# Attention followed by a routed expert layer: the gathers of later experts placed ahead of the flushed weight loads, one tile turned by TensorE

## The chip, the cores and the metric

One core of one Trainium2 chip runs the whole program. The metric is the device time of one execution in microseconds; the median of three executions is compared. The profile is of one further execution of the same program.

## What is computed

The reference is attention with normalised queries and keys, followed by a layer of eight experts to which every token is sent by a hash of its id:

```python
q_n, k_n = rmsnorm(q, g_q), rmsnorm(k, g_k)           # q, k, v: 8 x 12 x 448 x 64
attn = softmax(q_n @ k_n.T / 8) @ v
x = attn.transpose(0, 2, 1, 3).reshape(3584, 768)
expert_idx = token_ids * 2654435761 % 8
for e in range(8):
    mask = expert_idx == e
    h = np.maximum(x[mask] @ w1[e], 0.0)               # w1[e]: 768 x 1024
    out[mask] = h @ w2[e]                              # w2[e]: 1024 x 768
```

## The kernel before

The first half is attention. It writes x to a scratch tensor in DRAM (x_scratch), and beside it the token table gidx is made: for each expert up to 480 row numbers in four tiles (three of 128 rows, the last of 96).

The second half, from some 160 us on, goes through the experts in order, in the loop at line 1264. For an expert e it does the following.

- Gather: `fetch` (line 1048) issues one indirect DMA on GpSimd for each of the four tiles, from x_scratch into a ring of eight slots in SBUF (kr in the profile, line 230). Experts of even number use slots 0 to 3, those of odd number 4 to 7. Expert 2 is fetched inside expert 0's second product (line 1248), expert e + 2 at the head of expert e's turn through the loop (line 1274).
- Turn: the rows must stand with the model dimension on the partitions. For experts 2 to 6 VectorE does it, in `turn_blocks` (line 1061, the instructions are on line 1072) with sixteen 32-row block transposes: twelve of 32 x 768 and four of 32 x 576, since the last tile has 96 rows. They are issued for expert e + 1 ahead of expert e's first product. Experts 0 and 1 are turned tile by tile by TensorE (`turn`, line 1055, and `put_xT`, line 238: six transposes to PSUM and one copy back), expert 7 by DMA transposes on SyncE (line 1080).
- First product, `gemm1` (line 991; matmuls on line 1002, the ReLU on ScalarE on line 1011): 48 matmuls of 480 columns.
- Second product, `gemm2` (line 1018; matmuls on line 1024): four tiles of 16 matmuls, each copied out of PSUM on line 1034 and scattered to the output by an indirect DMA on GpSimd (line 1037).
- Weights: `w_pieces` (line 1083) cuts an expert's weights into three pieces of w1 (512 KB each in SBUF) and two of w2 (768 KB each), and `w_next` (line 1102) issues the next ones on GpSimd (line 1105). At the end of expert e the rest of the queue is issued and the pieces of expert e + 4 are queued. For e of 1 and more two pieces are issued after the first product and one after each tile of the second; for e = 0 one each after tiles 2 and 3, and three at the end.

GpSimd carries out its instructions in the order in which they are written, so the order of gathers, weight pieces and scatters in the program is the order in which they are issued. The two halves are scheduled by hand: what the plans `plan`, `before` and `between` (lines 1244 to 1258) name for an expert and a tile is issued at that place. The weights of expert e + 4 use the buffers of expert e; two buffers hold turned rows of experts 1 to 7, and a separate one those of expert 0.

Of the kernel before, what the change touches and what calls it, by code (L numbers as in the profile page):

```python
# [20 lines left out]
def kernel(  # L21
# [16 lines left out]
    E = moe_w1.shape[0]  # L38
# [13 lines left out]
    LAST = FIT - 3 * P  # L52
    KT = CAP // P
# [175 lines left out]
    def gather(xg, idx, rows=N):  # L229
        nc.gpsimd.indirect_dma_start(  # L230
            out=xg[0:idx.shape[0], :], out_offset=None, in_=x_dram[0:rows, :],
            in_offset=bass.IndirectOffsetOnAxis(ap=idx, axis=0),
            bounds_check=rows - 1, oob_is_err=False)
        return xg
# [729 lines left out]
    with tc.manual_schedule(), \  # L964
# [10 lines left out]
        def w1_view(e, w1_sb):  # L975
            return w1_sb[:].rearrange("p c (o f) -> p c o f" if e == 0 else "p c (f o) -> p c o f",
                                      o=FO)
# [13 lines left out]
        def gemm1(w1v, xT, h_sb, c0, c1, both=True, after=(), apart=0):  # L991
            banks = {}

            def products(fo, a0, a1):
                if fo not in banks:
                    banks[fo] = ps_h.tile([P, 512], FP32, name="h_ps")
                dst = banks[fo][:, a0 - c0:a1 - c0]
                if xT is xT_e:
                    dst = dst.rearrange("p (k t) -> p k t", t=P)
                for co in range(CO):  # L1000
                    src = xT[:, a0 // P:a1 // P, co, :] if xT is xT_e else xT[:, co, a0:a1]
                    nc.tensor.matmul(dst, lhsT=w1v[:, co, fo, :], rhs=src,  # L1002
                                     start=(co == 0), stop=(co == CO - 1))

            for fo in range(apart):
                products(fo, c0, c1 - P)
            for fo in range(FO):
                products(fo, c1 - P if fo < apart else c0, c1)
                h_ps = banks.pop(fo)
                if fo % 2 == 0 or not both:  # L1010
                    nc.scalar.activation(h_sb[:, fo, c0:c1], h_ps[:, :c1 - c0], AF.Relu)  # L1011
                else:
                    nc.vector.tensor_scalar(out=h_sb[:, fo, c0:c1], in0=h_ps[:, :c1 - c0],
                                            scalar1=0.0, scalar2=None, op0=ALU.max)
                for f in after[fo] if after else ():
                    f()
# [31 lines left out]
        def fetch(e, kts):  # L1048
            for kt in kts:
                c = e * KT + kt  # L1050
                xgs[c] = gather(xg_ring[:, c % (2 * KT)],
                                gidx[0:P if kt < KT - 1 else LAST, c:c + 1],
                                N_EARLY if kt < KT - 1 else N)

        def turn(e, kt, copy=None):
            if e not in xTs:
                xTs[e] = m_x.tile([P, CO, CAP], FP16, name="xT")
            bank = ps_x.tile([P, DIN], FP16, name="xT_ps")
            put_xT(xgs.pop(e * KT + kt), xTs[e], kt, bank[:], copy)

        def turn_blocks(e):
            xT = xTs[e] = m_x.tile([P, CO, CAP], FP16, name="xT")
            c0 = e * KT % (2 * KT)
            xg = xg_ring[:, c0:c0 + KT].rearrange("p k (c m r) -> p k m c r", m=4, r=32)
            dst = xT[:].rearrange("p c (g r) -> p c g r", r=32)
            for kt in range(KT):
                xgs.pop(e * KT + kt)
            for i in range(4):
                n = KT if 32 * i < LAST else KT - 1
                g = slice(i, i + 4 * (n - 1) + 1, 4)  # L1070
                for m in range(4):
                    nc.vector.transpose(  # L1072
                        out=dst[32 * m:32 * m + 32, :, g].rearrange("p c k r -> p k c r"),
                        in_=xg[32 * i:32 * i + 32, 0:n, m])

        def turn_by_dma(e):
            xTs[e] = m_x.tile([P, CO, CAP], FP16, name="xT")
            for kt in range(KT):
                n = P if kt < KT - 1 else LAST
                nc.sync.dma_start_transpose(out=xTs[e][:, :, kt * P:kt * P + n],  # L1080
                                            in_=xgs.pop(e * KT + kt)[0:n, :])
# [20 lines left out]
        def w_next(n):  # L1102
            for _ in range(min(n, len(queue))):
                o, i = queue.pop(0)
                nc.gpsimd.dma_start(out=o, in_=i)  # L1105
# [135 lines left out]
        def each(f, *parts):  # L1241
            return [lambda p=p: f(p) for p in parts]
# [3 lines left out]
            (0, "g", 4): [p7, p8], (0, "g", 5): [p9, p10, p11],  # L1246
            (0, "g", 6): each(low, 0, 1), (0, "g", 7): each(low, 2, 3), (0, "k", 0): [high],
            (0, "k", 1): [high_tok], (0, "k", 2): [table_mm, lambda: fetch(2, range(KT))],
            (1, "k", 0): [overflow_table],
        }  # L1250
        t = lambda e, kt: (lambda: turn(e, kt))
        t0 = lambda e, kt: (lambda: turn(e, kt, nc.scalar.copy))
        before, between = {}, {}
# [2 lines left out]
        before[0, 2] = [lambda: gemm1_late(w1_view(0, w_tiles[0][0]), xTs.pop(0), hs[0], EARLY, FIT)]  # L1256
        between[0, 2] = t0(1, 2)
        before[0, 3] = [t(1, 3)]
        hs = {}
        fetch(0, [KT - 1])  # L1260
        fetch(1, [KT - 1])
# [2 lines left out]
        for e in range(E):  # L1264
            w1_sb, w2_sb = w_tiles[e]
            h_sb = hs[e] = m_h.tile([P, FO, CAP], FP16, name="h_sb")
            after = [plan.get((e, "g", fo), []) for fo in range(FO)]
            if e == 0:
                gemm1(w1_view(e, w1_sb), xTs[e], h_sb, 0, EARLY, False, after, 2)
            else:  # L1270
                if e == E - 2:
                    turn_by_dma(E - 1)
                if e < E - 2:
                    fetch(e + 2, range(KT))
                    turn_blocks(e + 1)
                gemm1(w1_view(e, w1_sb), xTs.pop(e), h_sb, 0, FIT, e >= E - 2, after)
            if e:
                w_next(2)
            if e == 2:
                n_ov = nc.values_load(novi[0:1, 0:1], min_val=0, max_val=NOV)  # L1280
            if e == E - 1:
                nc.gpsimd.drain()
            for kt in range(KT):
                c = e * KT + kt
                for f in before.get((e, kt), []):
                    f()
                gemm2(w2_sb, h_sb, kt, gidx[:, c:c + 1], between=between.get((e, kt)),
                      last=(c == E * KT - 1), by_v=e in (0, E - 2, E - 1))
                for f in plan.get((e, "k", kt), []):
                    f()  # L1290
                if e or kt > 1:
                    w_next(1)
            w_next(len(queue))
            if e + 4 < E:
                queue += w_pieces(e + 4)
# [47 lines left out]
```

## Time and profile before

| | us |
|---|---|
| median of 3 runs | 331.68 |
| lowest and highest | 331.52, 332.45 |
| the profiled execution | 332.74 |
| its span, first to last instruction | 331.1 |

| engine | busy, us | share of the span |
|---|---|---|
| TensorE, matmuls | 318.2 | 96% |
| VectorE | 239.3 | 72% |
| ScalarE | 207.5 | 63% |
| GpSimd | 149.5 | 45% |

The 1.6 us by which the profiled execution is longer than its span lie ahead of the first and behind the last instruction. TensorE's busy time is modelled at the ends of matmuls, so 96% is not 96% of its peak; its granted clock is 0.994 over the span. The shares are means over the attention and the expert phase, whose limits differ; the change lies in the second.

### The profile page before, as it was taken

Reading aid. Unit: us, or ns where it says so; the run is one execution under the profiler, and the core shown is the slowest. Engines: PE = TensorE matmul, PEld = TensorE weight load, DVE = VectorE, ACT = ScalarE, POOL = GpSimd, SP = SyncE. Lnnn points to the kernel's source line nnn. Section 1 sums busy time; section 2 is a strip of 40 time slices with the busy share of each in tenths; the row PEclk is TensorE's granted clock in tenths of the full one; section 3 lists DMA queues with packets and bytes.
Section 4 is the critical chain, followed back from the end, with each engine's and each line's share of the span. In section 5 each row is a group of like instructions: output and inputs, shape, how many; then the busy total and the mean of one; then the engine's idle time right before and its main releaser. Section 6 shows DMA issues by size and latency. Waiting matters only on the chain. (4 is left out here: it accounts for less than half of the span.)

```text
span 331.1 us, 8985 instructions
## 1 busy us (share of the span) xinstructions
PE 318.2 (96%) x3765; PEld 219.7 (66%) x3765; DVE 239.3 (72%) x457; ACT 207.5 (63%) x317; POOL 149.5 (45%) x207
## 2 busy tenths in 40 slices
PE   7699999999999999999999999999999999999992
PEld 3467777777777777666767766666676675766761
DVE  4689999898999999985694397693958939422210
ACT  4699999999999999999543333424334253321211
POOL 8799944432441100003475872655727556403122
PEclk9999999999999999999999999999999999999997
DMA  6999999999999999722478699999999999993013
GB/s 122 197 202 203 194 242 196 236 200 240 203 240 212 245 225 227 164 70 70 124 152 211 165 207 242 244 264 265 265 272 239 254 253 260 307 174 137 23 48 124
DMA packets 45601, 65.52 MB, mean 198 GB/s; under 512 B 12727, under 2 KB 33423, under 8 KB 45432
## 3 DMA queue, kind: packets, MB, share of 16 engines
q0 software_dynamic: 39072, 58.32, 87.7%
q1 hardware_dynamic: 6328, 6.50, 7.5%
q8 instruction: 30, 0.49, 0.6%
q10 hardware_dynamic: 160, 0.11, 0.1%
q14 instruction: 11, 0.09, 0.1%
HBM read 89.29 MB, written 17.30 MB: 322 GB/s over the span
## 5 line engine op out<-in xcount | busy, mean ns | idle before, releaser
L660 ACT ACTIVATE expT<-sc_ps 128x896 bf16<-128x896 f32 x144 | 125.1, 960 | 1.0 <-PE sc_ps L637 0.7
L1072 DVE STREAM_TRANSPOSE xT<-kr 32x768 f16<-32x768 f16 (+1 forms) x80 | 73.6, 920 | 25.7 <-DMA kr<-x_scratch,gidx 15.2
L1024 PEld LDWEIGHTS <-h_sb 128*128 128x128 f16 (+1 forms) x512 | 52.2, 104 | 31.3
L1024 PE MATMUL o_ps<-w_sb,h_sb 128*128 128x512 f16 (+3 forms) x384 | 64.2, 326 | 0.0
L1011 ACT ACTIVATE h_sb<-h_ps 128x480 f16<-128x480 f32 (+1 forms) x56 | 31.3, 560 | 48.6 <-PE h_ps L1002 48.6
L1037 POOL DMA_INDIRECT out_dram<-o_sb,gidx x32 | 35.1, 1097 | 57.6 <-ACT o_sb L1034 29.6
L1034 ACT COPY o_sb<-o_ps 128x768 f32<-128x768 f32 (+1 forms) x26 | 20.8, 799 | 54.5 <-PE o_ps L1024 54.5
L230 POOL DMA_INDIRECT kr<-x_scratch,gidx x32 | 32.6, 1020 | 49.3 <-DVE qT L629 37.1
L1002 PEld LDWEIGHTS <-w_sb 128*128 128x128 f16 x300 | 39.8, 135 | 16.4 <-issue 0.7
L1002 PE MATMUL h_ps<-xT,w_sb 128*128 128x480 f16 x240 | 49.4, 366 | 0.3 <-DVE xT L1072 0.3
L637 PE MATMUL sc_ps<-qT,kT 64*128 64x448 f16 x288 | 44.4, 356 | 0.5 <-DVE qT L629 0.4
L678 PEld LDWEIGHTS <-expT 128*128 128x128 bf16 x846 | 36.8, 97 | 9.2 <-DVE x_sb L738 4.4
L678 PE MATMUL av_ps<-v,expT 128*128 128x65 bf16 x828 | 41.5, 193 | 0.1
L306 POOL DMA_DIRECT2D vr<-in_v_dram x36 | 23.7, 670 | 20.8 <-DMA kr<-in_k_dram 11.5
L738 DVE TENSOR_TENSOR x_sb<-av_ps,srec 128x448 f16<-128x448 f32 x47 | 29.3, 623 | 1.3
L663 ACT ACTIVATE expT<-sc_ps 128x448 bf16<-128x448 f32 x48 | 28.4, 595 | 0.1
L387 PEld LDWEIGHTS <-ident 128*128 128x128 f16 x576 | 22.6, 98 | 8.7 <-issue 4.4
L683 PE MATMUL av_ps<-v,expT 128*128 128x130 bf16 x138 | 24.0, 220 | 0.0
L1024 PE MATMUL o_ps<-kr,h_sb 128*128 128x512 f16 (+3 forms) x128 | 21.1, 326 | 0.0
L1002 PE MATMUL h_ps<-xT,qr 128*128 128x480 f16 x96 | 19.8, 366 | 0.5 <-DVE xT L1072 0.5
L637 PEld LDWEIGHTS <-kT 64*128 64x128 f16 x288 | 12.3, 93 | 9.5 <-issue 2.2
L1105 POOL DMA_DIRECT2D w_sb<-in_moe_w_dram x20 | 13.7, 692 | 9.4 <-DMA w_sb<-in_moe_w_dram 6.8
(226 smaller groups left out, 409.4 us busy)
## 6 DMA issues: line engine op xcount, KB each, us to landing
w_sb<-in_moe_w_dram POOLq DMA_DIRECT2D x18, 512.0 KB, 12.5
w_sb<-in_moe_w_dram POOLq DMA_DIRECT2D x8, 768.0 KB, 12.7
kr<-in_k_dram POOLq DMA_DIRECT2D x7, 672.0 KB, 15.6
qr<-in_q_dram POOLq DMA_DIRECT2D x7, 672.0 KB, 12.9
x_scratch<-x_sb SPq DMA_DIRECT2D x15, 288.0 KB, 6.4
w_sb<-in_moe_w_dram POOLq DMA_DIRECT2D x2, 1536.0 KB, 21.3
qr<-in_moe_w_dram POOLq DMA_DIRECT2D x6, 512.0 KB, 17.6
vr<-in_v_dram POOLq DMA_DIRECT2D x14, 192.0 KB, 13.6
```

The costliest lines, as they stand in the source:

```text
L230: nc.gpsimd.indirect_dma_start(out=xg[0:idx.shape[0], :], out_offset=None, in_=x_dram[0:rows, :], in_offset=bass.IndirectOffsetOnAxis(ap=i ...
L637: nc.tensor.matmul(sc[:, hh, :S], lhsT=kT[64 * hh:64 * hh + 64, P * j:P * j + P], rhs=qT[64 * hh:64 * hh + 64, :], start=True, stop=True)
L660: nc.scalar.activation(expT[:, 2 * j:2 * j + 2, :], sc[:, :, :S], AF.Exp, bias=0.0, scale=1.0)
L663: nc.scalar.activation(expT[:, 6, :], sc[:, 0, :S], AF.Exp, bias=0.0, scale=1.0)
L678: nc.tensor.matmul(av[:, 2 * t + hh, :], lhsT=expT[:, tl(hh, j), P * t:P * t + P], rhs=v8[:, i, vs(hh, j), 0:D + 1], start=(hh == 0 and t ...
L683: nc.tensor.matmul(av[:, 2 * t:2 * t + 2, :], lhsT=expT[:, 6, P * t:P * t + P], rhs=v8[:, i, 0::7, 0:D + 1], start=False, stop=False)
L738: nc.vector.tensor_tensor(out=xs[b][:, :, hp * D:hp * D + D], in0=av[:, :, :D], in1=srec[:, :, None].to_broadcast([P, SL, D]), op=ALU.mult)
L1002: nc.tensor.matmul(dst, lhsT=w1v[:, co, fo, :], rhs=src, start=(co == 0), stop=(co == CO - 1))
L1011: nc.scalar.activation(h_sb[:, fo, c0:c1], h_ps[:, :c1 - c0], AF.Relu)
L1024: nc.tensor.matmul(o_ps[d0 > 0][0:w, d0:d1], lhsT=h_sb[:, fo, col * P:col * P + w], rhs=w2_sb[:, fo, d0:d1], start=(fo == 0), stop=(fo == ...
L1037: scat = nc.gpsimd.indirect_dma_start(out=out[:, :], out_offset=bass.IndirectOffsetOnAxis(ap=idx[0:w], axis=0), in_=o_sb[0:w], in_offset=N ...
L1072: nc.vector.transpose(out=dst[32 * m:32 * m + 32, :, g].rearrange("p c k r -> p k c r"), in_=xg[32 * i:32 * i + 32, 0:n, m])
```

## The change

Four things are changed, all in the expert phase.

- Expert 3 is fetched by the plan after the last tile of expert 0's second product, ahead of the four weight pieces of expert 3 that are still to be issued there, instead of at the head of expert 1.
- Experts 4 to 7 are fetched in the expert before that which fetched them until now, after its second product and ahead of the flush of the weight queue.
- Expert 1 no longer issues two weight pieces after its first product; what is left over goes out at its flush.
- Of expert 2 three tiles are turned by VectorE (sixteen block transposes of 32 x 576); the fourth is turned by TensorE ahead of tile 2 of expert 1's second product, with the copy on ScalarE.

```diff
--- before.py
+++ after.py
@@ -1058,15 +1058,15 @@
             bank = ps_x.tile([P, DIN], FP16, name="xT_ps")
             put_xT(xgs.pop(e * KT + kt), xTs[e], kt, bank[:], copy)
 
-        def turn_blocks(e):
+        def turn_blocks(e, tiles=KT):
             xT = xTs[e] = m_x.tile([P, CO, CAP], FP16, name="xT")
             c0 = e * KT % (2 * KT)
             xg = xg_ring[:, c0:c0 + KT].rearrange("p k (c m r) -> p k m c r", m=4, r=32)
             dst = xT[:].rearrange("p c (g r) -> p c g r", r=32)
-            for kt in range(KT):
+            for kt in range(tiles):
                 xgs.pop(e * KT + kt)
             for i in range(4):
-                n = KT if 32 * i < LAST else KT - 1
+                n = tiles if 32 * i < LAST else min(tiles, KT - 1)
                 g = slice(i, i + 4 * (n - 1) + 1, 4)
                 for m in range(4):
                     nc.vector.transpose(
@@ -1246,6 +1246,7 @@
             (0, "g", 4): [p7, p8], (0, "g", 5): [p9, p10, p11],
             (0, "g", 6): each(low, 0, 1), (0, "g", 7): each(low, 2, 3), (0, "k", 0): [high],
             (0, "k", 1): [high_tok], (0, "k", 2): [table_mm, lambda: fetch(2, range(KT))],
+            (0, "k", 3): [lambda: fetch(3, range(KT))],
             (1, "k", 0): [overflow_table],
         }
         t = lambda e, kt: (lambda: turn(e, kt))
@@ -1256,6 +1257,7 @@
         before[0, 2] = [lambda: gemm1_late(w1_view(0, w_tiles[0][0]), xTs.pop(0), hs[0], EARLY, FIT)]
         between[0, 2] = t0(1, 2)
         before[0, 3] = [t(1, 3)]
+        before[1, 2] = [t0(2, KT - 1)]
         hs = {}
         fetch(0, [KT - 1])
         fetch(1, [KT - 1])
@@ -1271,10 +1273,9 @@
                 if e == E - 2:
                     turn_by_dma(E - 1)
                 if e < E - 2:
-                    fetch(e + 2, range(KT))
-                    turn_blocks(e + 1)
+                    turn_blocks(e + 1, KT if e > 1 else KT - 1)
                 gemm1(w1_view(e, w1_sb), xTs.pop(e), h_sb, 0, FIT, e >= E - 2, after)
-            if e:
+            if e > 1:
                 w_next(2)
             if e == 2:
                 n_ov = nc.values_load(novi[0:1, 0:1], min_val=0, max_val=NOV)
@@ -1290,6 +1291,8 @@
                     f()
                 if e or kt > 1:
                     w_next(1)
+            if e and e + 3 < E:
+                fetch(e + 3, range(KT))
             w_next(len(queue))
             if e + 4 < E:
                 queue += w_pieces(e + 4)
```

## Rows read from the trace of the kernel before

**Rows 1.** Timeline of TensorE: start, length (us), engine, line, work, idle before and releaser

```profile
180.09 0.42 PE L242 MATMUL xT_ps<-ident,kr 96*128 96x96 f16 x6
180.34 2.77 PE L1024 MATMUL o_ps<-w_sb,h_sb 128*96 128x512 f16 x16
...
192.66 10.56 PE L1024 MATMUL o_ps<-w_sb,h_sb 128*128 128x512 f16 x64
203.75 9.88 PE L1002 MATMUL h_ps<-xT,qr 128*128 128x480 f16 x48 [0.52 <-DVE xT L1072]
...
224.37 9.88 PE L1002 MATMUL h_ps<-xT,w_sb 128*128 128x480 f16 x48 [0.34 <-DVE xT L1072]
...
244.55 9.88 PE L1002 MATMUL h_ps<-xT,w_sb 128*128 128x480 f16 x48
...
264.72 9.88 PE L1002 MATMUL h_ps<-xT,w_sb 128*128 128x480 f16 x48
...
284.86 9.88 PE L1002 MATMUL h_ps<-xT,qr 128*128 128x480 f16 x48
294.58 10.56 PE L1024 MATMUL o_ps<-kr,h_sb 128*128 128x512 f16 x64
304.98 9.88 PE L1002 MATMUL h_ps<-xT,w_sb 128*128 128x480 f16 x48
```

**Rows 2.** Timeline of VectorE's turns, and its grouped row of the smaller form

```profile
209.41 14.91 DVE L1072 STREAM_TRANSPOSE xT<-kr 32x768 f16<-32x768 f16 x16 [4.30 <-ACT h_sb L1011]
...
229.58 14.92 DVE L1072 STREAM_TRANSPOSE xT<-kr 32x768 f16<-32x768 f16 x16 [5.26 <-DMA kr<-x_scratch,gidx]
249.75 14.92 DVE L1072 STREAM_TRANSPOSE xT<-kr 32x768 f16<-32x768 f16 x16 [5.25 <-PE h_ps L1002]
...
L1072 DVE STREAM_TRANSPOSE xT<-kr 32x576 f16<-32x576 f16 x4 | 3.1, 772 | 0.1
```

**Rows 3.** Two laps by windows: length, busy us (x instructions), clock, DMA share, GB/s

```profile
224.37:244.55 20.18, 20.18 (x112) 13.47 (x112) 14.72 (x16) 7.50 (x12) 11.60 (x13) 1.00 1.07 265
244.55:264.72 20.17, 20.17 (x114) 13.48 (x112) 14.72 (x16) 7.76 (x12) 11.58 (x13) 1.00 1.07 256
```

**Rows 4.** Gathers (line 230) in 191 to 197, then 234.5 to 240.5; time to landing

```profile
L230 POOL DMA_INDIRECT kr<-x_scratch,gidx x4: 988/1007/1077, 191.9 to 195.9; - x4
...
DMA to landing us min/median/max: 13.3/15.1/15.9
...
L230 POOL DMA_INDIRECT kr<-x_scratch,gidx x4: 975/1004/1077, 234.9 to 239.1; - x4
...
DMA to landing us min/median/max: 10.4/11.4/12.2
```

**Rows 5.** Timeline of GpSimd around the end of expert 0

```profile
186.85 0.81 POOL L1105 DMA_DIRECT2D w_sb<-in_moe_w_dram  x1
187.97 0.99 POOL L1037 DMA_INDIRECT out_dram<-o_sb,gidx  x1 [0.30 <-issue]
188.94 2.63 POOL L1105 DMA_DIRECT2D w_sb<-in_moe_w_dram  x4
191.87 1.08 POOL L230 DMA_INDIRECT kr<-x_scratch,gidx  x1 [0.30 <-issue]
...
195.88 0.99 POOL L230 DMA_INDIRECT kr<-x_scratch,gidx  x1 [0.30 <-issue]
```

**Rows 6.** Windows of 1 us at the start of the weights, columns as above

```profile
188.00:189.00 1.00, 1.00 (x6) 0.72 (x5) 0.22 (x1) 0.57 (x1) 1.00 (x2) 1.00 0.88 60
189.00:190.00 1.00, 1.00 (x6) 0.72 (x5) 0.99 (x2) 0.57 (x1) 1.00 (x2) 1.00 0.82 147
190.00:191.00 1.00, 1.00 (x6) 0.72 (x5) 0.99 (x2) 0.57 (x1) 1.00 (x3) 1.00 1.13 195
```

**Rows 7.** The page's DMA issues: count, KB each, median us to landing

```profile
w_sb<-in_moe_w_dram POOLq DMA_DIRECT2D x18, 512.0 KB, 12.5
w_sb<-in_moe_w_dram POOLq DMA_DIRECT2D x8, 768.0 KB, 12.7
```

## The prediction, made before the change was built

> **What bounds the kernel now.** I read the engines' timeline of the expert phase first, then what ended each wait, then the DMA rows. TensorE looks solid: it runs one expert as 48 matmuls of the first product and 64 of the second. The last two experts give the length of each half when nothing holds it: 294.58 - 284.86 = 9.72 us for the first, 304.98 - 294.58 = 10.40 us for the second, so 20.12 us for an expert [rows 1]. Against that the first products of experts 2 and 3 begin 0.52 and 0.34 us late, with "DVE xT L1072" as releaser [rows 1]. The laps after them, 244.55 - 224.37 = 20.18, then 20.17 and 20.14, are longer than 20.12 as well, with no idle time shown.
>
> VectorE's rows say why. Each turn of an expert is 16 transposes, 14.92 us, and the turns that begin at 209.41, 229.58 and 249.75 end at 224.32, 244.50 and 264.67: each time 0.05 us ahead of the first product that reads them [rows 1, 2]. A matmul that follows the end of a turn by the same 0.05 us three times is released by it; the records only hide the wait where it is shorter than the matmul pipeline. So from expert 3 to expert 6 the pace is set by the turns, and the question is what starts a turn. The gathers of expert 5 are issued up to 239.1 and the last lands 10.4 us later, at 249.5; the turn starts at 249.75. For expert 3 it is 195.9 + 13.3 = 209.2 against 209.41 [rows 2, 4]. The turns wait for gathered rows, although only the turn at 229.58 names the DMA as its releaser: the two others name engines whose work nothing in the turn needs at that moment, and the landings decide.
>
> And the rows wait for the DMA queue. One lap moves five weight pieces (3 x 512 KB and 2 x 768 KB [rows 7]), 480 gathered rows of 1536 B and 480 output rows of 3072 B: 5232 KB, 5.36 MB. The window of expert 3 moved 265 GB/s x 20.18 us = 5.35 MB at a DMA share of 1.07, the next one the same at 256 GB/s [rows 3]. The DMA engines are full, a lap of their work is as long as a lap of the kernel, and a gather lands when the work issued before it is done: 10.4 to 15.9 us after its issue [rows 4]. The bound of this stretch is therefore the DMA backlog, by a hair ahead of TensorE. It ends with the first product of expert 6 at 284.86; from there 331.1 - 284.86 = 46.2 us of TensorE work and the last store follow.
>
> **The change, part by part.** *Which gathers really move.* A queue of five pieces is emptied by two issues ahead of the second product and one after each of its four tiles, so for experts 2 to 4 nothing is left at the flush, and the gathers of experts 5 to 7 keep their place between the same scatters and the same weight pieces. What moves: the gathers of expert 3 pass four weight pieces (all of expert 3's but the first), the gathers of expert 4 pass one 768 KB piece, and two pieces of expert 4 go from ahead of expert 1's first two scatters to behind them.
>
> *TensorE's turn of one tile of expert 2.* Adds six transposes, 180.34 - 180.09 = 0.25 us [rows 1], on TensorE's path. Takes a quarter off VectorE's turn: 16 instructions of the smaller form, 16 x 0.772 = 12.4 us instead of 14.92 [rows 2]. The turn before ended 0.05 us ahead of 203.75; from the same start it now ends 2.57 us sooner, at 201.1, and it no longer needs the fourth gather. The added ScalarE copy of 96 rows is hidden: ScalarE is busy 7.5 us in a lap of 20.2 [rows 3], and the copy has from 198 to 203.3. If it were not hidden, the first product of expert 2 would wait, and the paragraph on expert 5 shows that up to 2 us of that would vanish. So that product begins at 192.66 + 10.40 + 0.25 = 203.31 instead of 203.75: 0.44 us won.
>
> *Expert 3.* Its gathers, issued from 189.3 to 194 with little ahead of them, land well before 200. The turn is then free to start when VectorE is; it needs to start by 223.43 - 0.05 - 14.92 = 208.46 only, and VectorE is done with expert 2 some 7 us before that. The first product of expert 3 begins at 203.31 + 20.12 = 223.43 instead of 224.37: 0.94 us won.
>
> *Expert 4.* Its rows land earlier by the 768 KB piece passed (786 kB at 260 GB/s, between the two windows of [rows 3], is 3.0 us) and later by whatever the queue has lost, below 1.3 us: 229.5 - 3.0 + 1.3 = 227.8, turned by 242.9. TensorE wants them at 243.55. So 244.55 becomes 243.55, 1.00 us won.
>
> *Expert 5, where it is decided.* The rows of expert 5 have the same work ahead of them as before: all weights of 3, 4 and 5, all scatters, the rows of 3 and 4. Reordering inside a queue that is always full doesn't move its end. It moves only if the queue runs dry at some time when it didn't before, and the changed order does that. Before, GpSimd issues the first piece of expert 3 at 186.85, a scatter at 187.97, then at 188.94 four pieces in 2.63 us, and the gathers afterwards, 191.87 to 196.87 [rows 5]. The DMA rate climbs from 60 GB/s (188 to 189) and 147 (189 to 190) to 195 (190 to 191), with the share over 1 from there [rows 6]: from about 189.5 the queue is full, and stays so to the end of the weights. After, the four gathers take GpSimd from 188.94 on, 196.87 - 191.57 = 5.3 us, and the 2.56 MB of weights are issued from 194.24 instead of 188.94. A piece issued into a queue that is nearly empty reaches full rate as the first did, 189.5 - 186.85 = 2.65 us after its issue: at 196.9. So between 189.5 and 196.9, 7.4 us, the DMA engines have the first piece (524 kB), the scatter of 96 rows (295 kB) and the rows of expert 3 (737 kB), 1556 kB less some 130 kB moved before 189.5: 1426 kB, at 260 GB/s 5.5 us, and about 0.6 us worth of the new piece's own climb. The hole is 7.4 - 5.5 - 0.6 = 1.3 us.
>
> Its bounds: if the piece follows the gathers at full rate as soon as its first packets can come (I take 1.1 us after the issue, from the climb that begins in the second after 188 [rows 6]), work resumes at 195.3 and 0.3 us is lost; if the small rows also keep the engines only half used while GpSimd writes them, as the share of 0.82 to 0.88 at 147 and 60 GB/s suggests for a queue fed piecemeal [rows 6], 2.2 us. I take 1.3, because it rests on the same piece's own climb.
>
> From there the queue is full again, so every later landing is 1.3 us late: rows of expert 5 at 250.8, turned by 266.0; TensorE, ready for them at 263.67, waits 2.3 us, and all that was won (1.05 us by then) is gone with 1.3 us on top. Expert 6 begins at 286.2, as its rows are late by as much; expert 7 is turned by DMA transposes with room to 304.98 and doesn't matter.
>
> **The sum.** 331.1 + 1.3 = 332.4 us of span, on the profiled execution 332.74 + 1.3 = 334.0. That execution was 1.06 us above the median of the runs, so on the median 331.68 + 1.3 = 333.0 us, with the bounds 332.0 and 333.9.
>
> **The rivals.** *The hole closes (331.7 to 332.5).* The weights climb at once, or the rows of expert 3 spread over the hole, and the loss is between 0 and 0.8 us. Expert 5 is then still the gate and nothing is won, because its rows can't come sooner than the work ahead of them. For it: the lower bound of 0.3. Against: 5.3 us of GpSimd's time stand against some 2.8 us of transfer that fill them.
>
> *DMA has room (330.6).* This is the faster side. If the full share of [rows 3] is engines that wait rather than work, a late start of the weights is made up within the next laps, the rows of experts 5 and 6 land by 248.5 and 268.6, and TensorE keeps its own pace to the end: 1.06 us won, 331.68 - 1.06 = 330.6. It decides as soon as expert 5's rows land 1.05 us sooner than before. Against: the laps carry 256 and 265 GB/s and no more, though GpSimd has issued ten microseconds ahead. The Trainium skill speaks for this rival: "DMA: Bandwidth & Descriptors", section "Anatomy of one DMA", prices a transfer from GpSimd at 2.0 us plus its bytes over 436 GB/s. By that figure a lap's 5.36 MB would be an estimated 12.3 us of moving, there would be some 8 us of room in each lap, and the time would be 330.6. The trace disagrees, with 20.2 us for those bytes.
>
> *The change does nothing at its gate.* If the early gathers had to wait on GpSimd for something (their slots, last read before 182; the index table), the old order would return in effect: 331.7 with the 0.25 us of transposes absorbed at expert 5. It falls into the first rival's range and I count it there.
>
> **How the numbers follow.** Forecast case, loss of 0.8 to 2.2 us, 332.5 to 333.9: 0.63. Hole closes or nothing changes: 0.27. DMA has room: 0.08. More than 2.2 us lost: 0.02. About 0.3%, 1.0 us, is what a measurement here can tell from no change; a loss over 1.0 us is the forecast case without its lowest part (0.05) and with the 0.02: 0.60 slower. Within 0.3%: 0.05 + 0.27 = 0.32. Faster: 0.08. The range is 331.5 to 333.9: it leaves out the fast rival, a little of the first one and the extreme.
>
> **What would show it.** Right: idle time of TensorE ahead of experts 2, 3 and 4 gone; the first product of expert 2 at 203.3 and of 4 at 243.6; a wait of some 2.3 us for a turn ahead of expert 5, at 266, none elsewhere; the DMA share dipping between 193 and 197; the rows of expert 5 landing at 250.8. Wrong: no dip there, or a dip with the rows of expert 5 at 249.5 or sooner, which would mean that the queue wasn't the bound; or TensorE late ahead of expert 2, which would put the loss on the transposes or their copy.

## The result, and the profile after

The changed kernel takes 336.82 us (median of 335.35, 337.79 and 336.82) against 331.68 before: 1.0137 times, 95% interval 1.0092 to 1.0181, or 5.1 us slower. The forecast was 333.0 with a range up to 333.9. The profiled execution of the changed kernel is its shortest, 335.35 us with a span of 333.8.

The attention half ends at its own moment in each execution, so positions below are counted from the first product of expert 1: 182.94 in the trace of before, 181.48 in the trace after. From there to the first product of expert 6 before takes 101.92 us ([rows 1] hold the end, 284.86) and after takes 287.51 - 181.48 = 106.03. What follows is 46.28 us in both (331.14 - 284.86 and 333.79 - 287.51). The loss, 4.11 us in these two traces, lies in that stretch alone. (The two spans differ by less, 2.65 us, because the attention half of the trace after happens to be 1.46 us shorter. The 5.1 us between the medians rest on three executions each; the median of before in the later groups below was 332.48 to 333.72, so about 1 us of the 5.1 stands in no trace.)

The timeline of TensorE after (start, length in us, engine, line, work, count, and in brackets idle time before and its releaser), which answers to [rows 1]:

```profile
181.48 9.88 PE L1002 MATMUL h_ps<-xT,w_sb 128*128 128x480 f16 x48
191.20 5.36 PE L1024 MATMUL o_ps<-w_sb,h_sb 128*128 128x512 f16 x32
196.40 0.42 PE L242 MATMUL xT_ps<-ident,kr 96*128 96x96 f16 x6
196.65 5.37 PE L1024 MATMUL o_ps<-w_sb,h_sb 128*128 128x512 f16 x32
201.85 9.88 PE L1002 MATMUL h_ps<-xT,qr 128*128 128x480 f16 x48
...
221.97 9.88 PE L1002 MATMUL h_ps<-xT,w_sb 128*128 128x480 f16 x48
...
242.09 9.88 PE L1002 MATMUL h_ps<-xT,w_sb 128*128 128x480 f16 x48
...
265.70 11.57 PE L1002 MATMUL h_ps<-xT,w_sb 128*128 128x480 f16 x48 [3.32 <-DVE xT L1072]
277.11 10.56 PE L1024 MATMUL o_ps<-w_sb,h_sb 128*128 128x512 f16 x64
287.51 9.88 PE L1002 MATMUL h_ps<-xT,qr 128*128 128x480 f16 x48
```

Experts 2, 3 and 4 start without a wait and the laps are 20.12 us, as forecast. Then two things stand at 265.70: a wait of 3.32 us for the turn of expert 5, and a first product that takes 277.11 - 265.70 = 11.41 us where the same 48 matmuls take 9.72 elsewhere. VectorE's turns, which answer to [rows 2], say where the wait comes from:

```profile
186.42 12.52 DVE L1072 STREAM_TRANSPOSE xT<-kr 32x576 f16<-32x576 f16 x16 [3.79 <-DMA kr<-x_scratch,gidx]
200.16 14.92 DVE L1072 STREAM_TRANSPOSE xT<-kr 32x768 f16<-32x768 f16 x16
226.63 14.91 DVE L1072 STREAM_TRANSPOSE xT<-kr 32x768 f16<-32x768 f16 x16 [11.56 <-DMA kr<-x_scratch,gidx]
250.73 14.92 DVE L1072 STREAM_TRANSPOSE xT<-kr 32x768 f16<-32x768 f16 x16 [9.19 <-DMA kr<-x_scratch,gidx]
```

The turn of expert 5 begins at 250.73, 69.25 after the first product of expert 1; before it was 249.75 - 182.94 = 66.81. It waits for gathered rows, by name now, and they come 2.44 us later than before. The delay is already there when they are issued: GpSimd starts the last of these gathers 58.57 us after the first product of expert 1, before 56.19, having stood idle for 2.50 and 1.46 us just ahead of them with a weight piece as releaser; from issue to landing it is 10.5 to 12.3 us, before 10.4 to 12.2. GpSimd's timeline and windows of 1 us (length, then busy us of PE, PEld, DVE, ACT and POOL, clock, DMA share, GB/s), which answer to [rows 5] and [rows 6]:

```profile
187.81 1.04 POOL L230 DMA_INDIRECT kr<-x_scratch,gidx  x1 [0.30 <-issue]
...
191.76 0.98 POOL L230 DMA_INDIRECT kr<-x_scratch,gidx  x1 [0.30 <-issue]
192.75 2.70 POOL L1105 DMA_DIRECT2D w_sb<-in_moe_w_dram  x4
```

```profile
190.00:191.00 1.00, 1.00 (x7) 0.71 (x6) 0.99 (x2) 0.57 (x1) 0.69 (x2) 1.00 0.98 289
191.00:192.00 1.00, 1.00 (x6) 0.49 (x5) 0.97 (x3) 0.57 (x1) 0.69 (x2) 1.00 1.01 359
192.00:193.00 1.00, 1.00 (x7) 0.47 (x5) 0.99 (x2) 0.00 (x0) 0.99 (x2) 1.00 0.65 206
193.00:194.00 1.00, 1.00 (x10) 0.80 (x9) 0.99 (x2) 0.00 (x1) 1.00 (x2) 1.00 0.46 145
194.00:195.00 1.00, 1.00 (x6) 0.48 (x5) 0.99 (x2) 0.80 (x1) 1.00 (x3) 1.00 0.68 71
```

The hole is there, from 192 to 195: the four gathers are written out one every 1.3 us, their rows are moved at once (they land 3.2 to 5.7 us after their issue, before 13.3 to 15.9), and the DMA engines stand half idle until the weight pieces, issued from 192.75 on, have come up to speed.

The slow first product is TensorE's clock:

```profile
262.30:265.70 3.40, 0.08 (x1) 0.00 (x0) 3.29 (x5) 0.79 (x1) 1.52 (x2) 1.00 1.03 236
265.70:266.50 0.80, 0.80 (x4) 0.58 (x4) 0.00 (x0) 0.00 (x0) 0.00 (x0) 1.00 0.99 313
266.50:270.00 3.50, 3.50 (x10) 1.47 (x9) 0.00 (x0) 0.66 (x2) 1.14 (x2) 0.51 1.06 292
270.00:277.11 7.11, 7.11 (x37) 4.99 (x36) 6.15 (x7) 3.33 (x6) 5.72 (x7) 1.00 1.10 239
```

TensorE did nothing from 262.4 to 265.70 (busy 0.08 of 3.40 us), and less than a microsecond after it had begun again the granted clock fell to half (0.51 over 3.50 us, the 1.2 GHz level). 10 matmuls were issued in those 3.50 us, where 37 take 7.11 us at full clock. It cost 11.41 - 9.72 = 1.69 us. With the late rows that is 2.44 + 1.69 = 4.13 us, against the 4.11 measured.

### The profile page after: what moved, and what is told of

It is laid out like the page before. It is cut to its first block, busy times and chain, and to the rows that moved or that the text cites. A ratio compares the mean times of both kernels' runs of the same rounds, so it can differ in the third digit from the quotient of the medians.

```text
span 333.8 us, 8998 instructions
## 1 busy us (share of the span) xinstructions
PE 319.9 (96%) x3771; PEld 220.1 (66%) x3771; DVE 236.3 (71%) x457; ACT 207.7 (62%) x318; POOL 149.1 (45%) x207
## 3 DMA queue, kind: packets, MB, share of 16 engines
HBM read 89.29 MB, written 17.30 MB: 319 GB/s over the span
## 5 line engine op out<-in xcount | busy, mean ns | idle before, releaser
L1072 DVE STREAM_TRANSPOSE xT<-kr 32x768 f16<-32x768 f16 (+1 forms) x80 | 71.2, 890 | 30.9 <-DMA kr<-x_scratch,gidx 29.8
L1002 PE MATMUL h_ps<-xT,w_sb 128*128 128x480 f16 x240 | 51.1, 374 | 3.3 <-DVE xT L1072 3.3
L640 PE MATMUL sc_ps<-qT,kT 128*128 128x448 f16 x48 | 16.9, 353 | 0.4 <-ACT expT L660 0.4
## 6 DMA issues: line engine op xcount, KB each, us to landing
qr<-in_q_dram POOLq DMA_DIRECT2D x7, 672.0 KB, 12.2
vr<-in_v_dram POOLq DMA_DIRECT2D x14, 192.0 KB, 13.3
```

Of the source, the lines that this page charges most:

```text
L1002: nc.tensor.matmul(dst, lhsT=w1v[:, co, fo, :], rhs=src, start=(co == 0), stop=(co == CO - 1))
L1072: nc.vector.transpose(out=dst[32 * m:32 * m + 32, :, g].rearrange("p c k r -> p k c r"), in_=xg[32 * i:32 * i + 32, 0:n, m])
```

## The experiments

The theory: the whole loss comes from the order gathers-then-weights behind expert 0, which lets the DMA queue run dry once; every later landing is late by the hole, and the gate is expert 5. Rivals: the two weight pieces of expert 4 that expert 1 no longer issues after its first product; the transposes on TensorE; and for the slow product, that something else than the wait slowed it. Each run was timed beside the kernel before, on the same chip: 332.81 us for the first four, 332.56 for the next group, 333.72 and 332.48 for the later ones.

This table holds the readings, one trace each; times in us. "Share" is the DMA share in the 14 us from 4 to 18 us after the first product of expert 1; "turn" and "expert 6" are the starts of the turn of expert 5 and of the first product of expert 6, both counted from the first product of expert 1.

| kernel | share | turn | expert 6 | ratio to before, 95% |
|---|---|---|---|---|
| before | 1.00 | 66.81 | 101.92 | 1 |
| turn only | 0.99 | 67.68 | 102.77 | 0.9994 (0.997 to 1.0019) |
| two pieces first | 1.02 | 67.07 | 102.15 | 1.0002 (0.9974 to 1.0031) |
| after | 0.87 | 69.25 | 106.03 | 1.0137 (1.0092 to 1.0181) |
| after, again | 0.89 | 70.17 | 106.90 | 1.0124 (1.005 to 1.0198) |
| gathers of expert 3 only | 0.89 | 69.21 | 104.29 | 1.0095 (1.0055 to 1.0134) |
| two pieces back | 0.88 | 69.39 | 106.18 | 1.0108 (1.0058 to 1.0159) |
| wait filled | 0.87 | 69.44 | 104.52 | 1.0076 (1.0048 to 1.0105) |
| longer hole | 0.71 | 71.02 | 108.81 | 1.0135 (1.0071 to 1.0199) |

### The turn of one tile by TensorE, alone

```diff
 (kernel before)
+        before[1, 2] = [t0(2, KT - 1)]
-                    turn_blocks(e + 1)
+                    turn_blocks(e + 1, KT if e > 1 else KT - 1)
```

> The kernel before with one part of the change alone: the fourth tile of expert 2 is turned by TensorE, VectorE turns three; all gathers and weight pieces keep their places. Theory (the DMA queue sets when the rows of expert 5 land, and the change made a hole in that queue): the first product of expert 2 begins 0.4 us sooner, those of experts 4 to 6 as before, since their rows land as before; time within 0.3 us of before, ratio 0.999 to 1.001. Rival (the transposes on TensorE or their copy on ScalarE cost the time): first product of expert 2 later than before, time 2 to 5 us above before.

332.48 us, no difference. Expert 2 starts without a wait, as in the changed kernel, but the next products give it back, since the rows behind them come no sooner:

```profile
202.28 9.88 PE L1002 MATMUL h_ps<-xT,qr 128*128 128x480 f16 x48
...
223.38 9.88 PE L1002 MATMUL h_ps<-xT,w_sb 128*128 128x480 f16 x48 [0.81 <-DVE xT L1072]
...
244.13 9.88 PE L1002 MATMUL h_ps<-xT,w_sb 128*128 128x480 f16 x48 [0.48 <-DVE xT L1072]
```

The transposes cost nothing in the end and win nothing alone.

### The gathers of expert 3 ahead of the weights, alone

```diff
 (kernel before)
+            (0, "k", 3): [lambda: fetch(3, range(KT))],
-                    fetch(e + 2, range(KT))
+                    if e > 1:
+                        fetch(e + 2, range(KT))
```

> The kernel before with one part of the change alone: the gathers of expert 3 go ahead of the four remaining weight pieces of expert 3; the other gathers and all pieces keep their places. Theory (hole in the DMA queue): the DMA share falls to about one half for some 3 us around the late start of the pieces, the rows of expert 5 land 1.3 us later than before, the first product of expert 5 waits some 1.5 to 2.3 us for its turn, time 1 to 2 us above before if the wait is too short for the clock to fall, 2.5 to 4 us if it falls as it did after the change (a stretch at 0.5 of 3.4 us costs 1.7 us). Rival (the loss comes from the pieces and scatters of expert 1 that changed places): time as before or up to 0.5 us less.

336.89 us: this one move brings most of the loss. The share falls as in the changed kernel (0.89) and the turn of expert 5 starts at 69.21, 2.4 us late where 1.3 was expected. Since the gathers of expert 4 keep their place, the wait shows one expert earlier:

```profile
246.62 9.88 PE L1002 MATMUL h_ps<-xT,w_sb 128*128 128x480 f16 x48 [2.55 <-DVE xT L1072]
```

In this execution the product behind that wait ran at full clock (256.34 - 246.62 = 9.72 us). Its time, 334.95 us, is near the lowest of the kernel's executions (333.54 to 337.77); seven of the others, the long ones (336.71 to 337.77), show a mean granted clock of 0.987 to 0.992, against 0.996 here. That fits a fall of the clock in most of them; where in the execution it fell isn't shown, as only this one has a trace.

### Two weight pieces of expert 4 back to their old place

```diff
 (kernel after)
-            if e > 1:
+            if e:
                 w_next(2)
```

> The changed kernel with expert 1 again issuing two pieces after its first product, so that nothing is left at its flush and the gathers of expert 4 follow all pieces; the gathers of expert 3 stay early, the tile stays with TensorE. Landings in the changed kernel were late by 1.3 us at the end of expert 3's pieces and by 2.4 us at the rows of expert 5. Theory A (only the hole matters, the other 1.1 us came by chance or from the hole too): rows of expert 5 land 2.4 us late as in the changed kernel, time as there, 4 to 5 us above before. Theory B (a second loss of 1.1 us comes from expert 1's weight pieces alternating with scatters): rows of expert 5 land 1.3 us late, the wait is some 2.3 us, time 1.3 to 3 us above before.

336.48 us. The rival falls: with the two pieces back the share is still 0.88, the turn of expert 5 starts at 69.39, and expert 6 at 106.18. The wait stands ahead of expert 4 instead, whose rows are behind those two pieces again, and the clock falls there (0.50 from 247.80 to 251.20):

```profile
247.30 11.57 PE L1002 MATMUL h_ps<-xT,w_sb 128*128 128x480 f16 x48 [3.08 <-DVE xT L1072]
```

### Two weight pieces ahead of the gathers of expert 3

```diff
 (kernel after)
-            (0, "k", 3): [lambda: fetch(3, range(KT))],
+            (0, "k", 3): [lambda: (w_next(2), fetch(3, range(KT)))],
```

> The changed kernel with two of the four weight pieces of expert 3 issued ahead of its gathers, so that the queue has 5 us of weights to move while GpSimd writes the gathers. Theory (hole): the DMA share stays near 1 through that stretch, the 1.3 us lost there are won back, the rows of expert 5 land about 1.1 us later than before instead of 2.4, the wait ahead of expert 5 is 2.0 to 2.3 us instead of 3.3, time 1 to 2.8 us above before. Rival (the hole is not the cause, the loss arises in expert 1): wait and time as in the changed kernel, 4 to 5 us above before.

332.77 us, level with before, so better than the changed kernel by all that it had lost, and better than expected: the expectation left 1.1 us of the delay standing, and the turn of expert 5 is only 0.26 us later than before. GpSimd issues two 512 KB pieces at 187.97 and the gathers after them, and the DMA engines have that megabyte to move while the gathers are written. Where the changed kernel had 0.65, 0.46 and 0.68 the share is over 1:

```profile
191.97:192.97 1.00, 1.00 (x6) 0.43 (x5) 0.99 (x2) 0.50 (x1) 0.70 (x2) 1.00 1.05 203
192.97:193.97 1.00, 1.00 (x9) 0.69 (x8) 0.97 (x3) 0.00 (x0) 0.69 (x2) 1.00 1.13 190
193.97:194.97 1.00, 1.00 (x9) 0.61 (x7) 0.99 (x2) 0.47 (x1) 1.00 (x2) 1.00 1.05 174
```

What remains is one wait and no fall of the clock:

```profile
264.00 9.88 PE L1002 MATMUL h_ps<-xT,w_sb 128*128 128x480 f16 x48 [1.13 <-DVE xT L1072]
```

Nothing else is changed than the order of six DMA issues. So the loss comes from that order, and the share shows through what: with the queue kept full, the late rows and the slow clock are gone too.

### The wait filled with matmuls

The changed kernel was run once more beside the next two, unchanged:

> The changed kernel once more, beside the others of this job. Its rows of expert 5 landed 2.4 us later than before, counted from the first product of expert 1, and its first product of expert 5 took 11.4 us instead of 9.7 with the granted clock at 0.5 for 3.4 us of it, just after TensorE had waited 3.3 us. Theory: wait of 3 us or more ahead of expert 5 again, a stretch at 0.5 behind it, time 4 to 5 us above before. Rival (the fall of the clock came by chance): the wait again, no stretch at 0.5, time 2 to 2.5 us above before.

It took 336.66 us, with the wait at 3.42 us and the clock at 0.86 over the product behind it:

```profile
267.37 11.52 PE L1002 MATMUL h_ps<-xT,w_sb 128*128 128x480 f16 x48 [3.42 <-DVE xT L1072]
```

To see whether the idle time of TensorE makes the product slow, 15 matmuls that nothing reads stand ahead of expert 5's first product:

```diff
 (kernel after, ahead of gemm1 of expert 5)
+                if e == 5:
+                    fill = ps_h.tile([P, 512], FP32, name="h_ps")
+                    for i in range(15):
+                        nc.tensor.matmul(fill[:, 0:FIT], lhsT=w1_view(e, w1_sb)[:, 0, 0, :],
+                                         rhs=hs[e - 1][:, 0, 0:FIT], start=True, stop=True)
```

> The changed kernel with 15 added matmuls of 480 columns, 3.0 us of TensorE work whose result nobody reads, ahead of the first product of expert 5, where TensorE waits 3 us for its turn. Nothing else is changed. Theory (the wait itself costs 2.4 us and the fall of the clock that follows an idle TensorE another 1.7): the first product of expert 5 begins when it did, takes 9.7 us instead of 11.4, no stretch at 0.5 there, time 1.5 to 1.7 us below the changed kernel, 2 to 3 us above before. Rival (that product is slow for another reason, its operands or the memory): it takes 11.4 us again, time as the changed kernel or above.

```profile
262.90 3.20 PE L1280 MATMUL h_ps<-h_sb,w_sb 128*128 128x480 f16 x15
266.57 9.88 PE L1002 MATMUL h_ps<-xT,w_sb 128*128 128x480 f16 x48 [0.46 <-DVE xT L1072]
276.28 10.56 PE L1024 MATMUL o_ps<-w_sb,h_sb 128*128 128x512 f16 x64
```

335.19 us, 1.5 us under the changed kernel of the same group by the medians, though the intervals of the two ratios overlap. The trace shows it plainly: the product starts as late as in the changed kernel (84.41 us after that of expert 1, there 84.22, and 85.14 in the second trace), takes 9.71 us again, and the clock stays at 1.00. Over whole executions the mean granted clock is 0.990 to 0.998 in the ten of this kernel, 0.985 to 0.991 in the seven of the changed one. So it is the idle wait that brings the clock down, and that is a term of its own beside the late rows.

### A longer hole

```diff
 (kernel after)
-            (0, "k", 3): [lambda: fetch(3, range(KT))],
+            (0, "k", 3): [lambda: (fetch(3, range(KT)), pad())],
```

> The changed kernel with four memsets of a scratch tile on GpSimd (some 2 us) between the gathers of expert 3 and the weight pieces that follow them, so that the pieces start later still. Theory (what the DMA queue lacks there is passed on to the rows of expert 5 and so to the end, one for one): rows of expert 5 land later than in the changed kernel by the length of the memsets less what the queue still holds, 1.5 to 2.5 us, the wait ahead of expert 5 grows from some 3.2 to some 5 us, time 1.5 to 2.5 us above the changed kernel. Rival (the queue catches up, or the loss in the changed kernel comes from elsewhere): rows of expert 5 and time as in the changed kernel.

`pad` is four memsets on GpSimd. They take 2.29 us between the last gather and the four pieces, which go out 13.51 us after the first product of expert 1 (after: 192.75 - 181.48 = 11.27).

```profile
194.26 2.29 POOL L1248 MEMSET pad_t<- 128x512 f32 x4
196.50 2.67 POOL L1105 DMA_DIRECT2D w_sb<-in_moe_w_dram  x4
```

```profile
186.99:200.99 14.00, 14.00 (x86) 9.08 (x84) 12.86 (x18) 5.42 (x10) 11.99 (x16) 1.00 0.71 149
```

338.16 us, 1.5 us over the changed kernel beside it by the medians, though the intervals of the two ratios overlap; the trace, of its longest execution (339.68 us), shows the mechanism. The share over the 14 us is 0.71. Against the mean of the three kernels without a hole (1.00) that is 0.29 x 14 us of work left undone, at the full share of 1.07 3.8 us; the turn of expert 5 starts 71.02 - 67.19 = 3.8 us later than their mean. For the five kernels with the plain hole the same sum gives 0.12 x 14 / 1.07 = 1.6 us by the share, and 69.49 - 67.19 = 2.3 us by the mean start of the turn. So a deeper hole comes out as later rows at the gate, 50 us on; one for one isn't shown, since from the plain to the longer hole the share loses 2.2 us more and the rows come 1.5 us later. The product behind the wait is slower still:

```profile
268.98 12.59 PE L1002 MATMUL h_ps<-xT,w_sb 128*128 128x480 f16 x48 [3.65 <-DVE xT L1072]
```

### Filled, and the gathers earlier

If gathers cost nothing when the queue holds enough work, they can go earlier still. In this kernel two pieces go ahead of expert 3's gathers, and the gathers of experts 4 to 7 go out in the middle of the second product (after tile 2 or 3), ahead of the weight pieces of that stretch. A first form, with the gathers after tile 2 for every expert:

> The changed kernel with two of the four weight pieces of expert 3 ahead of its gathers (the hole filled), and with the gathers of experts 4 to 7 ahead of the last two or three pieces of the weights of that expert's round instead of ahead of the flush, where they really pass something. Theory (rows of an expert wait for the work issued ahead of them): the rows of experts 4, 5 and 6 land 5 to 10 us sooner, no turn is late, TensorE shows no idle time from the first product of expert 1 on and laps of 20.12 us, time 1.0 us below before (331.7 where before has 332.8). Rival (DMA rate falls when rows stand between the pieces, or the wait moves to the scatters): waits ahead of experts 5 or 6 remain, time as before or above.

It took 351.49 us and says nothing on the question: expert 4's gathers stood ahead of TensorE's turn of expert 2's fourth tile, which reads the slot they write, so that tile is turned from other rows and TensorE waits 17.81 us for them. The second form has them after that turn:

```diff
 (two pieces first)
+                if e and kt == (2 if e == 1 else 1) and e + 3 < E:
+                    fetch(e + 3, range(KT))
                 if e or kt > 1:
                     w_next(1)
-            if e and e + 3 < E:
-                fetch(e + 3, range(KT))
```

> The kernel e8 mended: there the gathers of expert 4 overwrote the slot that TensorE's turn of expert 2 still had to read, which made TensorE and the gathers wait for each other's order, 17.8 us; here they follow that turn. Two weight pieces ahead of expert 3's gathers, gathers of experts 4 to 7 ahead of two or three pieces each. Theory: no idle time of TensorE ahead of any first product, laps of 20.1 us, 100.9 us from the first product of expert 1 to that of expert 6 (101.9 before, 106.0 to 106.9 after the change), clock at 1.00 through the expert phase, time 1.0 us below before, ratio 0.997. Rival (rows between the pieces slow the queue): waits ahead of experts 5 or 6, ratio 1.000 or above.

333.6 us, ratio 1.000 (0.998 to 1.0019). To the first product of expert 6 it went as expected: 100.86 us, every lap from expert 2 on 20.12 and no wait. Then, in the traced execution (334.82 us, the longest of the twelve), 2 us were lost inside that product. The timelines of SyncE, ScalarE and TensorE there:

```profile
281.34 17.30 SPq L1080 DMA_TRANSPOSE xT<-kr  x4
...
289.28 0.80 ACT L1034 COPY o_sb<-o_ps 96x768 f32<-96x768 f32 x1 [5.90 <-DMA out_dram<-o_sb,gidx]
...
290.60 6.24 PE L1002 MATMUL h_ps<-xT,qr 128*128 128x480 f16 x30 [1.85 <-ACT h_sb L1011]
```

Expert 7's rows came early, so its DMA transposes on SyncE began early, beside the last weights and scatters: 17.30 us, where the kernel before has

```profile
289.04 6.11 SPq L1080 DMA_TRANSPOSE xT<-kr  x4
```

ScalarE stood idle for 5.90 us ahead of its copy of expert 5's last tile. Ahead of such a copy it is 1.80 us where no scatter is waited for, so the copy began 4.1 us late, for want of an output buffer that a scatter still held; its ReLUs came behind it, and TensorE waited for those. The kernel before with the early gathers alone (those of expert 3 at their old place, no tile by TensorE) did the same:

```diff
 (kernel before)
-                    fetch(e + 2, range(KT))
+                    if e == 1:
+                        fetch(3, range(KT))
...
+                if e and kt == 1 and e + 3 < E:
+                    fetch(e + 3, range(KT))
```

> The kernel before with its gathers of experts 4 to 7 placed after the second tile of the second product of the expert before, ahead of two or three weight pieces; expert 3's gathers and all turns as before. Theory: rows of experts 4 to 6 land 4 to 10 us sooner and their turns are no longer late, but those laps were only 0.02 to 0.06 us over TensorE's own 20.12, and the waits ahead of experts 2 and 3 (0.52 and 0.34 us) stay: 0.1 to 0.2 us less than before, ratio 0.999 to 1.000. Rival (in most executions the queue is later than in the one profiled and the rows of experts 5 and 6 cost more than their rows show): 0.5 to 1 us less than before, and fewer executions above 333.

334.55 us, ratio 1.0025 (0.9998 to 1.0052), with transposes of 16.12 us and 4.71 us of idle time ahead of the same copy. Whether the early rows of expert 7 are the cause was tested by putting them alone back:

```diff
 (filled and early)
-                if e and kt == (2 if e == 1 else 1) and e + 3 < E:
+                if e and kt == (2 if e == 1 else 3 if e == 4 else 1) and e + 3 < E:
```

> As the filled and early version, but the gathers of expert 7 go out behind the last tile of expert 4's second product, where the kernel before has them in effect; experts 3 to 6 stay early. If the 2.0 us lost inside expert 6's first product came from the early rows of expert 7 (their DMA transposes on SyncE met the last weights and scatters for 17.3 us and held the output buffers), then: laps of 20.12 up to expert 7, no wait inside expert 6, the transposes back at some 6 us, first product of expert 1 to that of expert 6 100.9 us, the tail behind it 46.3 us as before, time 1.0 us under the kernel before, ratio 0.997. If the loss has another cause (the gathers of expert 5 or 6, the weights of expert 7), the wait of some 1.8 us inside expert 6 stays and the ratio is 1.000.

```profile
288.18 6.74 SPq L1080 DMA_TRANSPOSE xT<-kr  x4
...
283.39 0.80 ACT L1034 COPY o_sb<-o_ps 96x768 f32<-96x768 f32 x1 [1.80 <-PE o_ps L1024]
...
283.14 9.88 PE L1002 MATMUL h_ps<-xT,qr 128*128 128x480 f16 x48
...
303.26 9.88 PE L1002 MATMUL h_ps<-xT,w_sb 128*128 128x480 f16 x48
```

331.46 us against 332.48 before, ratio 0.9969 (0.9949 to 0.9989): 1.0 us faster than the kernel before, as expected, and some 5 us faster than the change. The wait inside expert 6 is gone, and no lap from expert 2 on is over 20.12 us. This is the version that beats both.

So the early place of expert 7's gathers cost the 2 us, and GpSimd's rows say more of the way than the expectation did. There are five output buffers (line 970), so the copy of expert 5's last tile takes over the one of expert 4's third tile. With the gathers early, GpSimd issues that tile's scatter behind them, 93.94 us after the first product of expert 1; with the gathers late, at 86.97. It then lands about 11.2 us after its issue in the first case, when the copy begins, and 13.9 us in the second. The buffer came free late because the scatter was issued late, behind four gathers, and not because it was slower to land beside the transposes. The gathers of experts 5 and 6 do the same on a smaller scale in the filled and early kernel, with no transpose under way, and TensorE doesn't wait there: the copies of the last tiles of experts 3 and 4 begin 1.6 and 2.0 us late.

```profile
246.52 0.80 ACT L1034 COPY o_sb<-o_ps 96x768 f32<-96x768 f32 x1 [3.38 <-DMA out_dram<-o_sb,gidx]
...
267.04 0.80 ACT L1034 COPY o_sb<-o_ps 96x768 f32<-96x768 f32 x1 [3.78 <-DMA out_dram<-o_sb,gidx]
```

Whether the transposes add to the 4.1 us isn't shown.

## Why the prediction was wrong in its size

**The bound: right.** The expert phase hangs on gathered rows behind a full queue, by a hair ahead of TensorE. Where the rows came earlier (last version: the turn of expert 5 at 58.07 instead of 66.81) TensorE ran at its own 20.12; where they came later it waited for all of it. The rows of expert 5 have the same work ahead of them, as the forecast had it: from the first product of expert 1 to their turn the DMA engines move 238 GB/s x 66.81 us = 15.9 MB before and 233 x 69.25 = 16.1 MB after.

**Experts 2 to 4: right.** Won were 0.44, 0.94 and 1.00 us by forecast. Counted from expert 1, the first products stand at 20.37, 40.49 and 60.61 in place of 20.81, 41.43 and 61.61: the same three numbers. The third is luck in part: the turn of expert 4 ended only 0.55 us ahead of its product (226.63 + 14.91 = 241.54 against 242.09), and in the second trace of the changed kernel TensorE waits 0.57 us there and expert 4 stands at 61.35.

**The gate: right.** One wait in this trace, ahead of expert 5, for the turn. No wait at expert 6, and expert 7 unaffected.

**The hole: right in kind and place; the delay behind it too small.** This is the first step that failed, a term that was mis-sized. The forecast took the loss as 7.4 - 5.5 - 0.6 = 1.3 us (0.3 to 2.2) and let every later landing be late by it; the rows of expert 5 came 2.44 us late in this trace, and 2.3 us in the mean of five kernels with the hole. The idle time itself was nearly right: by the DMA share it is 1.6 us over the 14 us, and about 1.4 us over the whole way from the first product of expert 1 to the turn of expert 5, where the mean share is 1.02 in the three kernels without a hole and 1.00 in the five with it, of some 69 us. The other 0.7 to 0.9 us are time in which the engines were busy longer over the same work, and why stays open: single traces without a hole differ by nearly that much (66.81 to 67.68), and so do those with it (69.21 to 70.17). That the working moved everything at 260 GB/s, the rate of a mixed lap, doesn't explain it. Rows are faster (289 and 359 GB/s in the windows in which they land; at 320 GB/s the 737 kB fill 2.3 us and not 2.8), but the first piece is slower (209 and 195 GB/s from 196 to 198, when w1 pieces move; at 200 GB/s the 524 kB fill 2.6 us and not 2.0), and the two nearly cancel. (Two slips of the working change nothing in the sum: the four pieces are 2560 KB, so 2.62 MB and not 2.56, and the lap at 256 GB/s moved 5.16 MB, less than the one at 265.)

**The wait's price: a term that was missing.** This is the second step that failed. The forecast counted a wait of TensorE at its own length. Here 3.32 us of waiting were followed by 1.69 us of half clock, which the filled wait gave back. The Trainium skill has this: "TensorE: Matmul & The Clock Gate", section "HAM oscillation — how this bites in real kernels", says that waits for DMA can throttle the clock again, and puts the extra time at the throttled time x (1 - 1.2/2.4). The trace agrees: a clock of 0.51 over 3.50 us is 1.7 us of work at full clock left undone, and the product was 1.69 us longer. The sum put it at nothing, without a reason. With the forecast's wait of 2.3 us it was not plain that it would come at all, and the wait of 2.55 us above came without it; but a forecast that ends in a single wait of some microseconds on a TensorE that was solid before has to carry it as an upper end.

**The sum.** Forecast: 1.05 won, 2.3 of wait, 1.3 lost. Measured from the first product of expert 1: 1.05 won by expert 5, whose product then begins 265.70 - 242.09 - 20.12 = 3.49 us behind TensorE's own pace (3.32 of it shown as idle), and 1.69 of clock: 3.49 - 1.05 + 1.69 = 4.1 lost in the traces. The medians differ by 5.1 us, and by 4.1 us in the second comparison. The bounds failed for the same two reasons: the delay passed the hole's upper end (2.2), and nothing stood for the clock. The upper end with the clock added is 333.9 + 1.7 = 335.6, against medians of 336.82 and 336.66.

**The rivals.** *The hole closes:* it didn't. *The change does nothing at its gate:* the gathers followed the scatter on GpSimd with 0.30 us between them. *DMA has room:* the lap windows after the hole carry no more than before:

```profile
222.00:242.00 20.00, 20.00 (x114) 13.31 (x113) 14.71 (x16) 7.75 (x12) 10.05 (x11) 1.00 1.07 256
242.00:262.00 20.00, 20.00 (x114) 13.31 (x113) 11.12 (x12) 7.54 (x12) 11.56 (x13) 1.00 1.04 252
```

A queue with room would have made up 2.4 us in those 40. The 1.06 us that this rival named are real all the same. They were to be had by order and not by speed: gathers ahead of more of the queue, with the queue kept full. The forecast's remark that the rows can't come sooner than the work ahead of them was true, and that work could be chosen.

## What to carry to other kernels

Putting small, urgent DMAs ahead of large ones on one queue is worth its order only while something large is already under way: count how long the issuing engine takes to write the small ones, and leave that much transfer ahead of them. A queue that was always full and ran dry once didn't get the time back here; look for the hole some laps ahead of the wait that it ends in. Small DMAs moved ahead also push back what stood behind them: here the scatters of two tiles, whose buffers the next expert's copies need. And a wait that appears on a TensorE that never waited costs its length and, as here, can cost 1.7 us of throttled clock behind it.

## What the runs showed of the hardware that was not expected

- In the expert phase the granted clock fell to half after waits of TensorE of 3.08, 3.32, 3.42 and 3.65 us, and did not after waits of 1.13 and 2.55 us, in the profiled executions. The stretch at half clock cost 1.6 to 1.7 us in the first three and more in the longer hole, whose product took 12.42 us in place of 9.72. The length of one wait doesn't decide it alone: some 11 us into the attention half the clock was at 0.50 for about 3 us behind a wait of 1.55 us (trace of the filled and early kernel) and of 1.32 us (longer hole), and stayed at 1.00 behind one of 1.59 us (before).
- At a DMA share of 1 and a little over, the rate differs with what is moved: 359 GB/s (191 to 192) while gathered rows of 1536 B landed, 209 and 195 GB/s (196 to 198) while pieces of w1 moved, 252 to 265 GB/s in a mixed lap. So bytes over one rate don't tell how long a queue still lasts.
- Four DMA transposes of one expert took 6.1 us at the end of the weights and 17.3 us when they began 9 us earlier, counted from the first product of expert 1, beside weights and scatters.
